# Forward attention scores in PSUM tiles of three banks instead of two

## The chip, the cores and the metric

The kernel runs on one core of a Trainium2 chip. The metric is the device time of one execution in microseconds. The engines that matter here are TensorE (PE), VectorE (DVE), ScalarE (ACT), GpSimd (POOL) and the DMA queue of SyncE (SP). Each engine works through its own list of instructions in order; semaphores hold an instruction back until what it needs is there. PSUM, into which PE writes, has eight banks of 512 float32 numbers per partition.

## The reference

One transformer block with conditioned layer norms, forward and backward in one launch. Attention has 32 heads of 16 numbers over 2048 tokens; the dense block has an inner width of 1792 and a squared ReLU.

```python
h = _layernorm(x) * (1 + ca) + sa
x = x + ga * _A_ref(h, A_wqkv, A_wo)          # softmax attention
h = _layernorm(x) * (1 + cb) + sb
x = x + gb * _B_ref(h, B_w1, B_b1, B_w2, B_b2)
...
scores = jnp.einsum('bhqd,bhkd->bhqk', q, k) * Dh ** (-0.5)
p = _softmax(scores, axis=-1)
o = jnp.einsum('bhqk,bhkd->bhqd', p, v)
```

The kernel returns the output and the gradients of nine inputs.

## The kernel before

Up to about 42 us the kernel prepares norms and the first projections. Then comes the forward loop, to 995 us, which the change is in. After it come the last chunk's dense block and the backward attention loop (exponentials at L1600), which are not touched.

**The forward loop** runs over `NF` = 512 units, `funits`: four chunks of 512 queries (`qc`), in each of them eight groups of four heads (`hg`), in each of these 16 key tiles of 128 keys (`kt`). Sixteen units with the same chunk and heads are called a group here; there are 32.

`fscore(u)` makes the scores of one unit. Each head has its 16 dimensions in its own 32 rows of the tiles `kt_sb` and `qt_sb`, so one head is one matmul on a row group of PE (L576), with a score tile of 128 keys by 512 queries, one PSUM bank. Two heads share a PSUM tile `psST` of two banks; ACT then takes the exponential of the 1024 columns (L578) into `ET`. There are three `psST` tiles in turn, and four `ET` tiles of a whole unit each.

`fpv(u)` multiplies the exponentials with the values, four matmuls side by side into the columns of one tile `oacc` (L592). It is called two units behind the scores. At the last key tile DVE copies `oacc` out to `ostage` (L596).

**What else goes on in the loop** is put between the units by hand. All engines' instructions stand in the order in which the code calls them. In the first 130 units or so a table, `plan`, puts in the key, query and value projections (L812, L826, `key_norm`, `token_tile`) for later chunks and heads. From unit 140 on `step(u)` takes one piece of a generator, `dense_chunk`, which runs the dense block forward and backward for a finished chunk of queries: products with four matmuls a piece at L410 (14 pieces), L424 (14), L446 (16), L500 (16, closed by a bias matmul at L505), L532 (4), transposes at L348, and the chains of weight gradients at L233. All of these share one PSUM tile of one bank, `pm`, which DVE empties (L412, L427, L457, L507 and L510, L536, L251) before the next product may begin. `steady` gives PE two filler matmuls (L615) in units with no product. PE's order in a unit thus is: four scores, four PV matmuls, a product or fillers.

Loads of the next group's keys and queries go out on POOL's queue one per unit from key tile 4 on (`fload`); other transfers go out on SP's queue at unit numbers (`later`).

PSUM is full: three `psST` of two banks, one `oacc`, one `pm`.

Of the kernel before, what the change touches and what calls it, by code (L numbers as in the profile page):

```python
# [14 lines left out]
AF = mybir.ActivationFunctionType  # L15
ALU = mybir.AluOpType
AX = mybir.AxisListType
BF = dt.bfloat16
F32 = dt.float32

P = 128
# [7 lines left out]
SCALE = 0.25  # L29
# [5 lines left out]
def kernel(  # L35
# [8 lines left out]
    TT = n // P  # L44
# [8 lines left out]
    PE = nc.tensor  # L53
    DVE = nc.vector
    ACT = nc.scalar
# [91 lines left out]
    with ExitStack() as ph:  # L147
# [1 line left out]
        ffw = ph.enter_context(tc.tile_pool(name="ffw", bufs=1))  # L149
        cb = ph.enter_context(tc.tile_pool(name="phMc", bufs=1))  # L150
        att = ExitStack()
        ework = att.enter_context(tc.tile_pool(name="phCe", bufs=4))
        b2row = ffw.tile([1, D], BF, name="b2row")
        racc = ffw.tile([P, 5, D], F32, name="racc")
        pools = {}
# [24 lines left out]
        def later(lag, f, *args):  # L180
            due.append((unit[0] + lag, f, args))

        def run_due(everything=False):
            i = 0
            while i < len(due):
                if everything or due[i][0] <= unit[0]:
                    _, f, args = due.pop(i)
                    f(*args)
                else:
                    i += 1  # L190
# [363 lines left out]
        funits = [(qc, hg, kt) for qc in range(QC) for hg in range(HG) for kt in range(TT)]  # L554
        fh, fe, fcur, fdone, dense = {}, {}, {}, [], []

        def fload(qc, hg):
            i = hg % 2
            kt_sb, qt_sb = kts[i], qts[i]
            rows = list(row_loads(kt_sb, qkT_st[1], hg, slice(0, n)))  # L560
            rows += row_loads(qt_sb, qkT_st[0], hg, slice(512 * qc, 512 * qc + 512), m_st)
            for i, (to, fro) in enumerate(rows):
                later(i, POOL.dma_start, to, fro)
            run_due()
            fh[qc, hg] = (qt_sb, kt_sb)

        def fscore(u):
            qc, hg, kt = funits[u]
            qt_sb, kt_sb = fh[qc, hg]
            ET = ework.tile([P, 4, 512], BF, name="ET", tag="ET")  # L570
            fe[u] = ET
            for pair in range(2):
                ps = pools["s"].tile([P, 2, 512], F32, name="psST", tag="psST")
                for hi in range(2):
                    r = 32 * (2 * pair + hi)
                    PE.matmul(ps[:, hi, :], kt_sb[r:r + 32, kt * P:(kt + 1) * P], qt_sb[r:r + 32, :],  # L576
                              start=True, stop=True, tile_position=(r, 0))
                ACT.activation(ET[:, 2 * pair:2 * pair + 2, :], ps[:], AF.Exp, scale=SCALE)  # L578

        def fpv(u):  # L580
            qc, hg, kt = funits[u]
            if kt == 0:
                fcur["o"] = pools["o"].tile([P, 512], F32, name="oacc", tag="oacc")
                if hg == 0:
                    fcur["rr"] = ework.tile([H, 512], F32, name="rrows", tag="rrows", bufs=1)
                    fcur["ou"] = ework.tile([P, 4, HG, P], BF, name="O_un", tag="O_un", bufs=1)
            oacc = fcur["o"]
            ET = fe.pop(u)
            for hq in range(4):
                h = hg * 4 + hq  # L590
                lhsT = vaug[:, kt].rearrange("p h c -> p (h c)")[:, h * (DH + 1):h * (DH + 1) + 32]
                PE.matmul(oacc[32 * hq:32 * hq + 32, :], lhsT, ET[:, hq, :],  # L592
                          start=(kt == 0), stop=(kt == TT - 1), tile_position=(0, 32 * hq), skip_group_check=True)
            if kt == TT - 1:
                ostage = ework.tile([P, 512], F32, name="ostage", tag="ostage", bufs=1)
                DVE.tensor_copy(ostage[:], oacc[:])  # L596
                obf = ework.tile([P, 512], BF, name="obf", tag="obf", bufs=2)
                if u == NF - 1:
                    fcur["last"] = ostage
                    return  # L600
                if hg == HG - 1:
                    DVE.tensor_copy(obf[:], ostage[:])
                else:
                    POOL.tensor_copy(obf[:], ostage[:])
                for hq in range(4):
                    h = hg * 4 + hq
                    later(2, sp, fcur["rr"][h:h + 1, :], ostage[32 * hq + 16:32 * hq + 17, :])
                later(3, sp, fcur["ou"][:, :, hg, :], obf[:], True)
                if hg == HG - 1:
                    fdone.append((u + 7, qc, fcur["rr"], fcur["ou"]))  # L610

        def steady(u):
            if 0 <= u < NF and funits[u][2] < TT - 1:
                for _ in range(2):
                    PE.matmul(fcur["o"][0:DH, :], zeros[:], identb.unsqueeze(1).to_broadcast([P, 4, P]), start=False, stop=False,  # L615
                              tile_position=(0, 0), skip_group_check=True)
# [497 lines left out]
        NF = len(funits)  # L1114
# [4 lines left out]
        def step(u):  # L1119
            nonlocal wait, turn  # L1120
            ripe = dwq and not open_group[0] and u >= dwq[0][0]
            if wait > 0 or not dense:
                wait = max(0, wait - 1)
                if ripe:
                    next_chain()
                return
            if ripe and turn and ((len(dwq) > 14 and fqueue) or dwq[0][3]):
                turn = 0
                next_chain()
                return  # L1130
            turn = 1
            w = next(dense[0], -1)
            if w == -2:
                next_chain()
            elif w == -1:
                dense.pop(0)
                run_due(True)
                if not fqueue:
                    loads["L"] = chunk_loads(QC - 1)
            else:  # L1140
                wait = w
# [6 lines left out]
        plan_tasks()  # L1148
        stages = [*range(4, 14), *range(4), 30, 31, *range(14, 25)]
        with ExitStack() as ph2:  # L1150
            pools["s"] = ph2.enter_context(tc.tile_pool(name="psS", bufs=3, space=bass.MemoryType.PSUM))
            pools["o"] = ph2.enter_context(tc.tile_pool(name="psO", bufs=1, space=bass.MemoryType.PSUM))
            pools["mm"] = ph2.enter_context(tc.tile_pool(name="psM", bufs=1, space=bass.MemoryType.PSUM))
            with tc.manual_schedule(engines={PE.engine, ACT.engine, DVE.engine, SP.engine, POOL.engine}):
                fh[0, 0] = (qts[0], kts[0])
                for u in range(NF + 2):
                    unit[0] = u
                    run_due()
                    if u < NF:
                        if funits[u][2] == 4 and u + TT < NF:  # L1160
                            fload(*funits[u + TT][0:2])
                        fscore(u)
                    if 2 <= u:
                        fpv(u - 2)
                    if u % 4 == 2 and u // 4 < len(stages):
                        later_stage(stages[u // 4])
                    if u % 4 == 0 and 18 <= u // 4 < 32:
                        turn_weights(u // 4 - 18)
                    count, begun_group = products[0], open_group[0]
                    for f, args in plan.pop(u, ()):  # L1170
                        f(*args)
                    if u < NF - 4:
                        step(u)
                    elif dwq and u >= NF - 2:
                        next_chain()
                    if products[0] == count and not (begun_group or open_group[0]):
                        steady(u - 2)
                    if u >= NF - 7 and "L" in loads and "O" not in loads["L"]:
                        early_finish()
                    if u == NF:  # L1180
                        tiny = wk.tile([P, 1], F32, name="tiny", tag="tiny", bufs=1)
                        ACT.activation(tiny[:], onesf[:, 0:1], AF.Sqrt)
                    if not dense and fqueue and fdone and u - 2 >= fdone[0][0]:
                        fqueue.pop(0)
                        qc, rr, ou = fdone.pop(0)[1:]
                        ffinish(qc, rr, ou, chunk_loads(qc))
                while dense:
                    unit[0] += 1
                    run_due()
                    step(unit[0])  # L1190
# [357 lines left out]
    with ExitStack() as ph:  # L1548
        tpool = ph.enter_context(tc.tile_pool(name="phIt", bufs=3))
        ework = ph.enter_context(tc.tile_pool(name="phIe", bufs=4))  # L1550
# [193 lines left out]
        with tc.manual_schedule(engines={PE.engine, ACT.engine, DVE.engine, SP.engine, POOL.engine}):  # L1744
# [4 lines left out]
            for b in range(NU // 4 + 3):  # L1749
                toks, bank = order_t if on_pe(b - 1) else order_n  # L1750
                for tok in toks:
                    c, i = tok[0], int(tok[1:] or 0)
# [43 lines left out]
    with ExitStack() as ph:  # L1796
# [174 lines left out]
        with tc.manual_schedule(engines={PE.engine, ACT.engine, DVE.engine}):  # L1971
            for i in range(2):
                rsums.append(pst.tile([P, D], F32, name="rsumJ", tag="ptq"))
            for t in range(TT):
# [4 lines left out]
                if t in (3, 5, 7, 9):  # L1979
                    i = 4 + (t - 3) // 2  # L1980
# [11 lines left out]
            for b in range(3):  # L1992
                for ic in range(DC):
                    dwqkv(b, ic)
                    i = b * DC + ic
# [77 lines left out]
```

## Time and profile before

| what | value |
|---|---|
| median of three runs | 2478.51 us (2475.77 to 2486.17) |
| profiled execution | 2479.05 us, span 2477.3 us |
| mean granted TensorE clock | 0.986 |
| PE busy | 2320.3 us (94% of the span) |
| ACT busy | 2302.8 us (93%) |
| DVE busy | 1834.7 us (74%) |
| forward loop, first to last exponential | 42.4 to 994.6 us |
| in the loop (42 to 995 us): ACT, PE, DVE busy | 942.4, 867.9, 472.3 us |

The span is the time from the first to the last instruction in the profile; the rest of the execution's time lies around it. A line of a group of instructions gives: source line, engine, operation, what it writes and reads, shapes, how many; behind the first bar the busy time in us (overlapping instructions counted once) and the mean duration of one in ns; behind the second bar the idle time of the engine just before them in us, and what ended most of it. A line of a timeline gives: start in us from the span's beginning, duration, engine, source line, operation, tiles and shapes, how many were merged into the line, and in brackets the idle time before it with what ended it. [...]

### The profile page before, as it was taken

Reading aid. Unit: us, or ns where it says so; the run is one execution under the profiler, and the core shown is the slowest. Engines: PE = TensorE matmul, PEld = TensorE weight load, DVE = VectorE, ACT = ScalarE, POOL = GpSimd, SP = SyncE. Lnnn points to the kernel's source line nnn. Section 1 sums busy time; section 2 is a strip of 40 time slices with the busy share of each in tenths; the row PEclk is TensorE's granted clock in tenths of the full one; section 3 lists DMA queues with packets and bytes.
Section 4 is the critical chain, followed back from the end, with each engine's and each line's share of the span. In section 5 each row is a group of like instructions: output and inputs, shape, how many; then the busy total and the mean of one; then the engine's idle time right before and its main releaser. Section 6 shows DMA issues by size and latency. Waiting matters only on the chain.

```text
span 2477.3 us, 49960 instructions
## 1 busy us (share of the span) xinstructions
PE 2320.3 (94%) x19020; PEld 780.1 (31%) x19020; DVE 1834.7 (74%) x2375; ACT 2302.8 (93%) x3560; POOL 487.5 (20%) x660
## 2 busy tenths in 40 slices
PE   8899899989998998899999999999999999999999
PEld 3232233323322332442233233332232323323344
DVE  6555353455445554578999999999999999999985
ACT  7999999999999999639999999999999999999964
POOL 2211222432544352101111101101011010110100
PEclk9999999999998999999999999999999999999999
DMA  4478453266647765979999999999999999999995
GB/s 148 125 173 179 143 142 101 84 172 134 91 93 162 150 134 104 248 225 170 196 203 210 192 209 198 205 201 206 206 211 192 209 201 200 207 191 217 201 265 179
DMA packets 1190335, 438.22 MB, mean 177 GB/s; under 512 B 1068107, under 2 KB 1161225, under 8 KB 1189582
## 3 DMA queue, kind: packets, MB, share of 16 engines
q1 hardware_dynamic: 1153246, 389.87, 79.9%
q0 software_dynamic: 19872, 27.09, 6.7%
q10 hardware_dynamic: 16976, 18.07, 2.9%
q8 instruction: 149, 2.44, 0.4%
q14 instruction: 92, 0.75, 0.1%
HBM read 98.30 MB, written 70.80 MB: 68 GB/s over the span
## 4 chain that ended last, share of the span: by engine, by line
ACT 41%; PE 38%; issue 8%; DVE 8%; DMA 2%; ACTq 1%; POOL 0%; DVEq 0%; POOLq 0%
ACT E_u L1600 25%; ACT ET L578 12%; PE dqacc L1702 4%; PE psST L576 3%; PE psS_A L1594 3%; PE pm L233 2%; PE accVK L1675 2%; ACT dsT L1787 2%; PE psS_B L1594 2%; PE oacc L592 2%; PE pm L500 2%; PE pdh L1895 2%; PE pm L424 2%; PE psS_C L1594 2%; PE pm L410 2%
## 5 line engine op out<-in xcount | busy, mean ns | idle before, releaser
L1616 DVE TENSOR_TENSOR dS_u<-psD_u,E_u 128x1024 bf16<-128x1024 f32 x1024 | 1185.2, 1216 | 70.8 <-PE psD_u L1614 26.2
L578 ACT ACTIVATE ET<-psST 128x1024 bf16<-128x1024 f32 x1024 | 942.0, 1245 | 13.7 <-PE psST L576 13.3
L1600 ACT ACTIVATE E_u<-psS_A 128x512 bf16<-128x512 f32 x768 | 508.3, 662 | 10.8 <-PE psS_C L1594 8.1
L1600 ACT ACTIVATE E_u<-psS_B 128x512 bf16<-128x512 f32 x768 | 501.5, 653 | 10.1 <-PE psD_u L1614 3.0
L1614 PE MATMUL psD_u<-iv,ido 32*128 32x512 bf16 x2048 | 408.3, 386 | 1.2 <-DVE dS_u L1616 1.1
L576 PE MATMUL psST<-qt_sb,kt_sb 32*128 32x512 bf16 x2048 | 315.8, 386 | 45.5 <-ACT ET L578 40.7
L1600 ACT ACTIVATE E_u<-psS_C 128x512 bf16<-128x512 f32 x512 | 333.3, 651 | 2.3 <-PE psS_B L1594 0.9
L1594 PE MATMUL psS_B<-ik,iq 32*128 32x512 bf16 x768 | 294.2, 383 | 11.0 <-ACT E_u L1600 3.7
L1594 PE MATMUL psS_A<-ik,iq 32*128 32x512 bf16 x768 | 292.6, 381 | 11.4 <-DVE dwlast L237 0.9
L1723 POOL TENSOR_TENSOR dQacc<-dQacc,dqtmp 128x512 f32<-128x512 f32 x64 | 81.2, 1268 | 851.7 <-ACT dqtmp L1718 851.7
L1594 PEld LDWEIGHTS <-iq 32*128 32x128 bf16 x2048 | 130.4, 91 | 314.3 <-issue 296.9
L1675 PE MATMUL accVK<-dS_u,qz 128*32 128x512 bf16 x2048 | 213.4, 388 | 0.4 <-DVE dS_u L1616 0.2
L592 PE MATMUL oacc<-ET,vaug 128*32 128x512 bf16 x2048 | 206.9, 394 | 3.9 <-DVE ostage L596 3.9
L1684 PE MATMUL accVK<-E_u,dOs_tok 128*16 128x512 bf16 x2048 | 203.5, 386 | 0.0
L1594 PE MATMUL psS_C<-ik,iq 32*128 32x512 bf16 x512 | 193.5, 378 | 4.3
L576 PEld LDWEIGHTS <-kt_sb 32*128 32x128 bf16 x2048 | 85.1, 91 | 327.9 <-issue 308.0
L1702 PE MATMUL dqacc<-dsT,KS_tok 128*32 128x512 bf16 x2048 | 146.5, 383 | 14.8 <-DMA dsT<-dS_u 1.4
L251 DVE COPY part<-pm 128x512 f32<-128x512 f32 (+2 forms) x106 | 65.1, 614 | 119.3 <-PE pm L233 115.6
L1787 ACT ACTIVATE dsT<-ptT 128x1024 bf16<-128x1024 bf16 x126 | 142.6, 1132 | 6.5 <-PE ptT L1648 5.8
L1614 PEld LDWEIGHTS <-ido 32*128 32x128 bf16 x2048 | 105.5, 91 | 102.1 <-issue 96.0
L1675 PEld LDWEIGHTS <-qz 128*32 128x32 bf16 x2048 | 58.6, 94 | 177.6 <-issue 162.6
L592 PEld LDWEIGHTS <-vaug 128*32 128x32 bf16 x2048 | 53.1, 93 | 122.1 <-issue 122.1
(419 smaller groups left out, 2668.4 us busy)
## 6 DMA issues: line engine op xcount, KB each, us to landing
p_st<-part POOLq DMA_DIRECT2D x36, 256.0 KB, 4.7
kt_sb<-qkT_st POOLq DMA_DIRECT2D x124, 64.0 KB, 2.9
wA<-in_B_w_dram SPq DMA_DIRECT2D x28, 256.0 KB
wB<-w1T_st SPq DMA_DIRECT2D x21, 256.0 KB
wA<-w2T_st SPq DMA_DIRECT2D x21, 256.0 KB
wB<-in_B_w_dram SPq DMA_DIRECT2D x21, 256.0 KB
p_st<-part POOLq DMA_DIRECT2D x28, 192.0 KB, 4.8
p_st<-part SPq DMA_DIRECT2D x18, 256.0 KB
```

The lines of the kernel that those rows point to most:

```text
L576: PE.matmul(ps[:, hi, :], kt_sb[r:r + 32, kt * P:(kt + 1) * P], qt_sb[r:r + 32, :], start=True, stop=True, tile_position=(r, 0))
L578: ACT.activation(ET[:, 2 * pair:2 * pair + 2, :], ps[:], AF.Exp, scale=SCALE)
L592: PE.matmul(oacc[32 * hq:32 * hq + 32, :], lhsT, ET[:, hq, :], start=(kt == 0), stop=(kt == TT - 1), tile_position=(0, 32 * hq), skip_grou ...
L1594: PE.matmul(psS[:], st["q"][r:r + 32, qt * P:(qt + 1) * P], st["k"][r:r + 32, kc * 512:kc * 512 + 512], start=True, stop=True, tile_positi ...
L1600: ACT.activation(bst[u][0][:, hq, :], sst.pop((u, hq))[:], AF.Exp, scale=SCALE)
L1614: PE.matmul(psD[:, hi, :], st["do"][r:r + 32, qt * P:(qt + 1) * P], st["v"][r:r + 32, kc * 512:kc * 512 + 512], start=True, stop=True, til ...
L1616: DVE.tensor_tensor(dS_u[:, 2 * pair:2 * pair + 2, :], psD[:], E_u[:, 2 * pair:2 * pair + 2, :], ALU.mult)
L1675: PE.matmul(cur["vk"][32 * hq:32 * hq + 32, :], hst[hg]["qz"][:, qt, hq, :], bst[u][1][:, hq, :], start=(qt == 0), stop=False, tile_positi ...
L1684: PE.matmul(acc[32 * hq:32 * hq + DH, :], dOs_tok[:, qt, (hg * 4 + hq) * DH:(hg * 4 + hq + 1) * DH], E_u[:, hq, :], start=False, stop=(qt ...
L1702: PE.matmul(acc[32 * hq:32 * hq + 32, :], KS_tok[:, kc * 4 + kt, h * DH:h * DH + 32], tT[:, :, hq * 4 + kt, :], start=(kt == 0), stop=(kt ...
L1723: POOL.tensor_tensor(dst2, dst, tmp[:], ALU.add)
L1787: ACT.activation(dst, pt[:], AF.Identity)
```

## The change

The score tiles get three banks, and there are two of them. The scores of a group are 16 x 4 = 64 banks in order of key tile and head; they are cut into 22 slots, twice ten of three banks and one of two. A slot has one PSUM tile, one exponential and one `ET` tile of three banks (five of these in turn). A slot may hold heads of two neighbouring key tiles. The loop calls `fscore` once in every unit, and once more at the end of the units of key tiles 1, 4, 7, 10, 12 and 15, behind that unit's product. `fpv` of a unit is called inside `fscore`, once the unit's last slot is two slots back, at most one per slot; four of its matmuls read the unit's four heads from one or two `ET` tiles.

```diff
-        ework = att.enter_context(tc.tile_pool(name="phCe", bufs=4))
+        ework = att.enter_context(tc.tile_pool(name="phCe", bufs=5))
...
-        def fscore(u):
-            qc, hg, kt = funits[u]
+        widths = ([3] * 10 + [2]) * 2
+        first_tile = [sum(widths[:j]) for j in range(len(widths))]
+        doubles = (1, 4, 7, 10, 12, 15)
+        slot_ends = {}
+        fnext = {"slot": 0, "pv": 0}
+
+        def fscore():
+            s = fnext["slot"]
+            fnext["slot"] = s + 1
+            g, j = divmod(s, len(widths))
+            qc, hg, _ = funits[g * TT]
             qt_sb, kt_sb = fh[qc, hg]
-            ET = ework.tile([P, 4, 512], BF, name="ET", tag="ET")
-            fe[u] = ET
-            for pair in range(2):
-                ps = pools["s"].tile([P, 2, 512], F32, name="psST", tag="psST")
-                for hi in range(2):
-                    r = 32 * (2 * pair + hi)
-                    PE.matmul(ps[:, hi, :], kt_sb[r:r + 32, kt * P:(kt + 1) * P], qt_sb[r:r + 32, :],
-                              start=True, stop=True, tile_position=(r, 0))
-                ACT.activation(ET[:, 2 * pair:2 * pair + 2, :], ps[:], AF.Exp, scale=SCALE)
+            w = widths[j]
+            ET = ework.tile([P, 3, 512], BF, name="ET", tag="ET")
+            ps = pools["s"].tile([P, 3, 512], F32, name="psST", tag="psST")
+            for i in range(w):
+                kt, hq = divmod(first_tile[j] + i, 4)
+                r = 32 * hq
+                PE.matmul(ps[:, i, :], kt_sb[r:r + 32, kt * P:(kt + 1) * P], qt_sb[r:r + 32, :],
+                          start=True, stop=True, tile_position=(r, 0))
+                fe.setdefault(g * TT + kt, []).append(ET[:, i, :])
+                slot_ends[g * TT + kt] = s
+            ACT.activation(ET[:, 0:w, :], ps[:, 0:w, :], AF.Exp, scale=SCALE)
+            if fnext["pv"] < NF and len(fe.get(fnext["pv"], ())) == 4 and slot_ends[fnext["pv"]] <= s - 2:
+                fpv(fnext["pv"])
 
         def fpv(u):
+            fnext["pv"] = u + 1
...
-                PE.matmul(oacc[32 * hq:32 * hq + 32, :], lhsT, ET[:, hq, :],
+                PE.matmul(oacc[32 * hq:32 * hq + 32, :], lhsT, ET[hq],
...
-            pools["s"] = ph2.enter_context(tc.tile_pool(name="psS", bufs=3, space=bass.MemoryType.PSUM))
+            pools["s"] = ph2.enter_context(tc.tile_pool(name="psS", bufs=2, space=bass.MemoryType.PSUM))
...
-                        fscore(u)
-                    if 2 <= u:
-                        fpv(u - 2)
+                        fscore()
+                    elif u < NF + 1:
+                        while fnext["pv"] < NF - 1:
+                            fpv(fnext["pv"])
+                    else:
+                        fpv(NF - 1)
...
-                        steady(u - 2)
+                        steady(fnext["pv"] - 1)
+                    if u < NF and funits[u][2] in doubles:
+                        fscore()
```

## The prediction

> **What bounds the kernel now.** I read the page first (busy rows, then groups), then the waits inside the forward loop (42 to 995 us of the span), then the timeline of single units. A unit is one 128-key tile for four heads; the loop has 512 of them, 32 groups (head group and chunk) of 16. Nothing outside the loop is touched.
>
> ```profile
> PE   8899899989998998899999999999999999999999
> DVE  6555353455445554578999999999999999999985
> ACT  7999999999999999639999999999999999999964
> ```
>
> These rows of the page are tenths busy in 40 slices of 62 us. In slices 2 to 16 ACT is full, PE nearly, DVE half.
>
> ```profile
> L578 ACT ACTIVATE ET<-psST 128x1024 bf16<-128x1024 f32 x1024 | 942.0, 1245 | 13.7 <-PE psST L576 13.3
> L576 PE MATMUL psST<-qt_sb,kt_sb 32*128 32x512 bf16 x2048 | 315.8, 386 | 45.5 <-ACT ET L578 40.7
> ```
>
> ACT's 1024 exponentials fill 942 of 952 us; it idled 13.3 us for scores, and PE waited 40.7 us for ACT to free score tiles. ACT sets the loop, PE follows closely. The mean of 1245 ns is not the price of an exponential, since neighbours overlap. The price is read from PE's timeline where the loop runs on ACT alone:
>
> ```profile
> 262.51 0.39 PE L576 MATMUL psST<-qt_sb,kt_sb 32*128 32x512 bf16 x2 [0.37 <-ACT ET L578]
> ...
> 264.34 0.39 PE L576 MATMUL psST<-qt_sb,kt_sb 32*128 32x512 bf16 x2 [0.37 <-ACT ET L578]
> ...
> 266.18 0.39 PE L576 MATMUL psST<-qt_sb,kt_sb 32*128 32x512 bf16 x2 [0.37 <-ACT ET L578]
> ```
>
> The same score pair waits for ACT every 1.834 us, so one 1024-column exponential costs 0.917. For half the width I take the backward loop's unbroken ACT stretch:
>
> ```profile
> 1508.22 0.63 ACT L1600 ACTIVATE E_u<-psS_B 128x512 bf16<-128x512 f32 x1
> ...
> 1510.61 0.69 ACT L1600 ACTIVATE E_u<-psS_A 128x512 bf16<-128x512 f32 x1
> ```
>
> Ends lie 2.45 us and five instructions apart: 0.490 for 512 columns. Hence 0.427 per 512 columns, 0.063 fixed per instruction, and 0.917 + 0.427 = 1.344 for 1536 columns (estimate: no PSUM exponential of that width is in the trace).
>
> **Part 1, fewer exponentials: -20.2 us.** A group now has 32 x 0.917 = 29.34 us of exponentials; afterwards 20 x 1.344 + 2 x 0.917 = 28.71. Times 32: 320 fixed costs of 0.063 saved, 20.2 us, and the pace of a unit falls from 1.834 to 1.795. Bounds for the 1536-column price: 1.280 (no fixed cost) and 1.5 x 0.917 = 1.375 (nothing saved, 0 us in place of -20.2); I take 1.344, on the line through both measured widths.
>
> [...]
>
> **Part 2, the slack between PE and ACT.** A score tile may be refilled from 0.05 us after the exponential that empties it, and must be begun 0.49 before ACT needs it: after a stall, scores begun at 785.54 let ACT start at 786.03. The slack is (tiles - 1) exponentials less 0.54: now 2 x 0.917 - 0.54 = 1.29 us, afterwards 1.344 - 0.54 = 0.80. PE gets less even, too. A score burst takes 0.325 before the next kind of matmul starts, whether two or four matmuls are in it (they start 3 ns apart, on different row groups), so I take it for three; PV 0.326; four products 4 x 0.215 + 0.096 = 0.956. A unit with a product and one burst is 1.607 of PE work. In the built order the six extra slots of a group stand behind the products of key tiles 1, 4, 7, 10, 12 and 15, against the next unit's slot. So in a run of three units PE lags ACT by 3 x (1.607 - 1.344) = 0.79 and then gains it back: it fits into 0.80 with nothing over. A unit in which PE waits longer costs ACT time that is covered now.
>
> **Part 3, stages that give back.** (a) The product loop at L410:
>
> ```profile
> 805.95 0.40 PE L576 MATMUL psST<-qt_sb,kt_sb 32*128 32x512 bf16 x4
> 806.05 0.75 DVE L412 TENSOR_SCALAR rT<-pm,b1col 128x512 bf16<-128x512 f32 x1 [0.66 <-PE pm L410]
> 806.27 0.40 PE L592 MATMUL oacc<-ET,vaug 128*32 128x512 bf16 x4
> ...
> 806.86 1.02 PE L410 MATMUL pm<-h2T,wA 128*128 128x512 bf16 x4 [0.18 <-DVE rT L412]
> ...
> 807.81 0.39 PE L576 MATMUL psST<-qt_sb,kt_sb 32*128 32x512 bf16 x4
> ```
>
> The one product tile goes PE, DVE, PE in 1.866 us whatever ACT does; an extra burst hides in that wait (0.31 + 0.215 + 0.65 = 1.18 us from the last product matmul to the next, against 1.866 - 0.645 = 1.22 by way of the eviction). So 42 units (14 in each of three chunks) do not get faster: 42 x 0.039 = 1.6 us given back. (b) In the alternating L424 and L233 products units last 1.804 and 1.884, also paced by eviction: 64 units, 2.5 us. (c) L500, where two DVE reads free the tile late:
>
> ```profile
> 474.98 0.69 DVE L507 TENSOR_TENSOR gfprod<-pm,g_c 128x512 bf16<-128x512 f32 x1 [6.53 <-PE psST L576]
> ...
> 475.59 0.68 DVE L510 TENSOR_TENSOR ftmp<-pm,modbc 128x512 bf16<-128x512 f32 x1
> ...
> 476.32 1.02 PE L500 MATMUL pm<-wB,sT 128*128 128x512 bf16 x4 [0.40 <-DVE ftmp L510]
> ...
> 477.27 0.40 PE L576 MATMUL psST<-qt_sb,kt_sb 32*128 32x512 bf16 x4
> ```
>
> From 474.56 to 477.27 PE gives ACT nothing new; then three units of 1.63, 1.63 and 1.37 catch up, and ACT never runs dry (12 units in 22.04 us, 1.837 each). Walking the new slots through those 12 units with the prices above (next product 2.07 behind the last one at each tile change), ACT idles 0.36, 0.26, 0.61, 0.61 and 0.27, together 2.1 us, because 2.71 - 1.34 is beyond 0.80 and the extra slots take PE's time for catching up. 48 units: 8.4 us. The four L532 units that follow in each chunk are paced by eviction at up to 1.99: 1.0 us. (d) L446, five-unit cycles with one gap of 2.2: the same walk gives 0.8 us of idle in 15 units; 56 units: 3.0. (e) The first 51 units, where key, norm and value products wait on evictions: half the gain lost, 1.0. (f) ACT's own 13 stalls, where PE stands behind DVE or a transfer: two lie at the start; at each of the other 11 the slack is 0.49 less, and PE stands somewhere in its run, so 0 to 0.49 each; I take 0.4, near the end that full runs make: 4.4. Sum given back: 1.6 + 2.5 + 8.4 + 1.0 + 3.0 + 1.0 + 4.4 = 21.9.
>
> **Part 4, edits at nothing.** The exponential's ET tile is one of five with three banks instead of four with four; its readers, the PV of a unit whose last slot is two back, are issued behind the score two slots earlier, so it is free over an exponential before it is needed. If it were not, all later exponentials and the scores behind them would queue, 1.3 us a time. PV keeps its two units' distance and never waits for ACT, since the score ahead of it waited for the same exponential. SP's and POOL's orders are the old ones; the next group's key and query loads land in 2.9 us (median), the last of them is issued four units (7.3 us) ahead, and that lead shrinks by 4 x 0.04 us. The filler matmuls stay as many.
>
> **Sum.** 2479.05 (the profiled execution: span 2477.3 and 1.75 around it) - 20.2 + 21.9 = 2480.8, so 2481. That execution lies 0.5 us above the median of 2478.51; 0.5% of it, 12 us, is about what a measurement of this kernel can tell from no change.
>
> **Rivals.** *Slack suffices, faster.* If PE makes up at L500, L446 and the stalls what it loses, only the eviction-paced 1.6 + 2.5 + 1.0 go back: 2479.05 - 20.2 + 5.1 = 2464. For it: ACT is never dry at L500 now. Against it: 0.79 in 0.80. Chance 0.19.
>
> *The run overshoots, slower.* If a burst of three tiles costs PE or ACT's start 0.1 us more than a pair does, every run of three product units ends some 0.3 late instead of just in time. That decides from bursts over 0.33 on. Some 380 units carry products, about 220 of them outside (a) to (d): 82 runs, of which a late one leaves the next half relieved, 0.2 each: 16 us more, 2497. For it: nothing is left over in the window, and only bursts of two and of four have been seen. Against it: those cost the same. Chance 0.24. [...]
>
> *Three scores do not run side by side, much slower.* At 0.215 more per slot a group of products needs 22 x 0.54 + 16 x (0.326 + 0.956) = 32.4 of PE against 29.3 now; over some 18 such groups 56 us: 2535. Against it: four start within 10 ns of each other at 805.95. Chance 0.04.
>
> *The fixed cost is larger, much faster.* An exponential after idle lasts 1.02 from start to end (786.03), 0.164 over its columns; were that the price, 320 x 0.164 = 52 saved, 2449. Against it: the 1.834 cycle. [...] Chance 0.02.
>
> **How the numbers follow.** The forecast keeps 0.51. Faster by over 0.5% (below 2466) are the first and last rival, 0.21; slower by over 0.5% (above 2491) the two middle ones, 0.28; within it 0.51, with its own range of 2467 to 2490 (terms c, d and f between half and one and a half). The range reaches from the first rival to the second, and up to the bound where a wide exponential saves nothing (2501): 2463 to 2500.
>
> **What would show it.** Ends of wide exponentials 1.34 apart. ACT's idle on psST in the loop rising from 13 to some 30 us, most of it at L500 and behind stalls. L410 units still 1.87. The light units around 261 us at 1.80. The last exponential within 5 us of 994.6. A loop that ends before 982 refutes part 3; one after 1006, or score bursts over 0.33, shows the second or third rival.

## The result, and the profile after

The changed kernel takes 2502.71 us in the median of seven runs (2492.82 to 2506.6), the kernel before 2478.51 (2472.83 to 2489.76). The ratio is 1.008, with a 95% interval of 1.005 to 1.0109: slower by 0.5 to 1.1%. The profiled execution took 2506.1 us with a span of 2504.3, so it lies in the upper part of the seven; it is 27.05 us above the profiled execution of before. It also has the lowest mean granted clock of the seven, 0.979; the four at 0.985 to 0.988 took 2492.82 to 2502.71.

All of this is in the forward loop. From the first to the last exponential it lasts from 41.6 to 1023.8 us, 982.1 us against 952.2, which is 29.9 more; what follows lasts 1480.5 us against 1482.6, and the loop begins 0.8 earlier.

The busy rows of the changed kernel's page, tenths in 40 slices of 63 us, with the granted TensorE clock:

```profile
PE   8888789888988898899999999999999999999999
ACT  7999999989999999646999999999999999999964
PEclk9999899999999999999999999999999999999999
```

ACT, which was at 9 in slices 2 to 16, now drops to 8 in the ninth slice, its light stretch at the loop's end is a slice longer, and PE has more slices at 8. The fifth digit of the clock is an 8.

The two groups of the loop on the same page; behind the second bar stands the engine's idle time:

```profile
L589 ACT ACTIVATE ET<-psST 128x1536 bf16<-128x1536 f32 (+1 forms) x704 | 933.5, 1443 | 52.1 <-PE psST L585 49.9
L585 PE MATMUL psST<-qt_sb,kt_sb 32*128 32x512 bf16 x2048 | 278.1, 393 | 81.9 <-ACT ET L589 75.0
```

ACT idled 49.9 us for scores where it had been 13.3, and PE waited 75.0 us for ACT where it had been 40.7. Both wait longer for each other: with two tiles each has less in hand when the other is late. The list of waits in the loop (42 to 1025 us; total, times, longest) says how often:

```profile
PE psST L585 <- ACT ET L589: 75.0, 154, 1.0
ACT ET L589 <- PE psST L585: 49.9, 91, 3.5
```

ACT ran dry 91 times instead of 13 (gaps over 0.15 us). The longest case is 3.5 us as before, so what is new is many short gaps.

Where the loop runs on ACT alone, the timeline of the changed kernel shows the price of the wide exponential:

```profile
262.38 0.39 PE L585 MATMUL psST<-qt_sb,kt_sb 32*128 32x512 bf16 x3 [0.43 <-ACT ET L589]
...
263.73 0.39 PE L585 MATMUL psST<-qt_sb,kt_sb 32*128 32x512 bf16 x3 [0.20 <-ACT ET L589]
...
265.07 0.39 PE L585 MATMUL psST<-qt_sb,kt_sb 32*128 32x512 bf16 x2 [0.20 <-ACT ET L589]
...
266.41 0.40 PE L585 MATMUL psST<-qt_sb,kt_sb 32*128 32x512 bf16 x3 [0.95 <-ACT ET L589]
```

Each slot waits for the release of a tile, 1.35, 1.34 and 1.34 us apart. Over all ends of back-to-back exponentials the interval is 1.3425 for 1536 columns and 0.9165 for 1024.

With these prices the loop's account can be drawn up. I call lost time what the ends of the exponentials lie apart beyond the price of each. Before, 13.6 us were lost in the loop; afterwards 64.2. So 20.2 us were saved, 50.6 more were lost, and the difference is 30. The clock records divide the lost time: before, 7.2 us fell into stretches in which TensorE was granted half its clock (with 2 us behind each) and 6.4 outside; afterwards 21.3 and 42.9. By the 22 slots of a group, counted from 0, lost time stands mostly at slots 2, 6, 10, 13, 14 and 21 (4.3, 7.8, 7.4, 7.4, 7.1 and 8.5 us of the 64.2): five of these are extra slots, issued behind a product.

### The profile page after: what moved, and what is told of

Same layout as the page of the kernel before. It is cut to its first block, busy times and chain, and to the rows that moved or that the text cites. A ratio compares the mean times of both kernels' runs of the same rounds, so it can differ in the third digit from the quotient of the medians.

```text
span 2504.3 us, 49831 instructions
## 1 busy us (share of the span) xinstructions
PE 2299.9 (92%) x19020; PEld 775.5 (31%) x19020; DVE 1833.5 (73%) x2375; ACT 2293.4 (92%) x3240; POOL 487.8 (19%) x660
## 5 line engine op out<-in xcount | busy, mean ns | idle before, releaser
L589 ACT ACTIVATE ET<-psST 128x1536 bf16<-128x1536 f32 (+1 forms) x704 | 933.5, 1443 | 52.1 <-PE psST L585 49.9
L585 PE MATMUL psST<-qt_sb,kt_sb 32*128 32x512 bf16 x2048 | 278.1, 393 | 81.9 <-ACT ET L589 75.0
L585 PEld LDWEIGHTS <-kt_sb 32*128 32x128 bf16 x2048 | 77.3, 91 | 336.9 <-issue 326.1
```

What stands on the lines that cost most here:

```text
L585: PE.matmul(ps[:, i, :], kt_sb[r:r + 32, kt * P:(kt + 1) * P], qt_sb[r:r + 32, :], start=True, stop=True, tile_position=(r, 0))
L589: ACT.activation(ET[:, 0:w, :], ps[:, 0:w, :], AF.Exp, scale=SCALE)
```

## The experiments

Three theories were put to the test. *Slack*: two tiles leave 0.80 us where three left 1.29, and extra slots behind products bring PE late by more. *Clock*: the half-speed stretches, twelve in place of five in the loop, cost the time. *Burst*: a second score burst in a unit, behind the product, costs PE time by itself.

**Two pair tiles.** The kernel before, with its third score tile taken away:

```diff
-            pools["s"] = ph2.enter_context(tc.tile_pool(name="psS", bufs=3, space=bass.MemoryType.PSUM))
+            pools["s"] = ph2.enter_context(tc.tile_pool(name="psS", bufs=2, space=bass.MemoryType.PSUM))
```

> The kernel before with two score tiles of two banks instead of three; nothing else. Slack theory: two tiles leave 0.917 - 0.54 = 0.38 us between PE and ACT instead of 1.29, so every unit with a product (1.607 us between score bursts) leaves ACT dry; the unit becomes about 2.1 us in the 380 product units, 2550 to 2600 us in all, ACT idle on scores over 70 us. Clock theory (the loss is half-speed windows of TensorE): nothing but the share of those windows counts, so near 2480 unless they become more. Burst theory (the extra score bursts cost PE time): bursts are as many as before, so 2480.

Measured: 2576.58 us, ratio 1.0396 (1.0337 to 1.0455), from two executions of 2567.23 and 2585.94; the profile is of the faster. The two groups on its page:

```profile
L578 ACT ACTIVATE ET<-psST 128x1024 bf16<-128x1024 f32 x1024 | 968.2, 1031 | 82.9 <-PE psST L576 76.6 <-ACT ET L578 0.2
L576 PE MATMUL psST<-qt_sb,kt_sb 32*128 32x512 bf16 x2048 | 373.1, 390 | 108.9 <-ACT ET L578 100.7 <-DVE vP L831 1.8
```

The same exponentials, and ACT idles 76.6 us for scores in place of 13.3; the loop lasts 1047.6. By the rule of the prediction the slack here is 0.917 - 0.54 = 0.38. Slack of 1.29, 0.80 and 0.38 goes with 13.6, 64.2 and 109.0 us lost: the number of tiles alone costs this much, and the wider tile buys back part of what the missing third tile costs.

**Extra slot first.** The changed kernel, with the second slot of a double unit scored right behind the first, so ahead of the unit's product:

```diff
                         fscore()
+                        if funits[u][2] in doubles:
+                            fscore()
...
-                    if u < NF and funits[u][2] in doubles:
-                        fscore()
```

> The changed kernel with the six extra slots of a group called right behind the unit's first slot, ahead of its product, instead of behind the product. Slack theory: the largest lag of a run falls from 0.79 to about 0.53 against 0.80, and at L410 the extra burst lies in the wait for the eviction; ACT's idle in the loop falls from 50 to 25 us and the time to about 2480. Clock theory: same number of half-speed windows, so as the changed kernel, 2492 to 2506. Burst theory: same number of bursts, so as the changed kernel.

Measured: 2487.64 us, ratio 1.0046 (1.0028 to 1.0064); the loop is 963.4. Of the 64.2 us lost, 18.8 are back by nothing but the order in which the same work stands on PE (15.1 by the medians; 12.2 of the 18.8 lie outside half-speed stretches). A time of about 2480 was expected. What remains gathers at slots 12 and 13, 20.2 us of 45.4, ahead of the extra slot of key tile 10.

**Four fillers.** The changed kernel with four filler matmuls in a unit without a product, so that PE works more:

```diff
-                for _ in range(2):
+                for _ in range(4):
```

> The changed kernel with four filler matmuls in place of two in units without a product (0.43 us more of PE work in such a unit, 1.61 between bursts, still under ACT's pace). Clock theory: PE is busier in the light stages, the half-speed windows in the loop fall from 12 towards the 5 of the kernel before, and 8 to 15 us come back. Slack theory: the product stages stay as they are; light units now lag as product units do, so the same or up to 5 us slower.

Measured: 2510.42 us, ratio 1.0127 (1.01 to 1.0154). There are six half-speed stretches in its loop (37.5 us) in place of twelve (64.9), and yet the loop is longer, 990.2, with 72.3 us lost. The 8 to 15 us that the clock theory expected back did not come: half as many stretches gained nothing that the fillers' own PE time did not take again. Since the fillers cost time of their own, this run alone does not price the clock; the executions at equal clock that are compared further down do. The granted clock is higher with more fillers, 0.987 in this profile against 0.979 (0.9865 against 0.985 in the median of the executions).

**Split pairs.** The kernel before, three tiles of two banks, with the second pair of a unit scored behind the product, where the changed kernel has its extra slots:

```diff
                         fscore(u, (0,))
...
+                    if u < NF:
+                        fscore(u, (1,))
```

> The kernel before, three tiles of two banks, but the second pair of a unit is scored behind the unit's product instead of right after the first pair: the bursts become as scattered as in the changed kernel (more so), the tiles and exponentials stay. Slack theory: the lag inside a unit is 1.607 - 0.917 = 0.69, within the 1.29 of three tiles; only stages where PE itself sets the pace (L500) pay for the extra burst, 3 x 0.215 us in four units: 2484 to 2490. Burst theory: 512 more bursts cost more than the 192 of the change did, 20 us or more: over 2500.

Measured: 2474.36 us, ratio 0.999 (0.9974 to 1.0005), lost time 11.6 us. With three tiles a score burst behind the product adds nothing to the loop (2484 to 2490 was expected even by the slack theory), and the burst theory, by which 512 more bursts cost 20 us or more, falls. That a burst takes PE time which only the slack of three tiles hides is not excluded.

**First and nine.** Extra slot first, and the double unit of key tile 9 in place of 10:

```diff
-        doubles = (1, 4, 7, 10, 12, 15)
+        doubles = (1, 4, 7, 9, 12, 15)
```

> extra_slot_first with the extra slot of key tile 10 moved to key tile 9, so that the extra slots stand 3, 3, 2, 3, 3, 2 units apart instead of 3, 3, 3, 2, 3, 2 with a two-bank slot ahead of the long gap. Slack theory: ACT's lost time at slots 12 to 14 of a group, 20 of 45 us in extra_slot_first, falls to the 8 of the other half of the group; 2472 to 2478. If only the number of tiles mattered and not the lag, no change: 2487.

Measured: 2479.54 us, ratio 1.0007 (0.9991 to 1.0022). The groups on its page:

```profile
L589 ACT ACTIVATE ET<-psST 128x1536 bf16<-128x1536 f32 (+1 forms) x704 | 928.7, 1452 | 31.2 <-PE psST L585 29.0
L585 PE MATMUL psST<-qt_sb,kt_sb 32*128 32x512 bf16 x2048 | 283.2, 389 | 68.9 <-ACT ET L589 62.7 <-DVE vP L845 1.8
```

The time is just above the 2472 to 2478 that were expected. ACT's idle time for scores is 29.0 us, the loop 956.4, lost time 38.5 (11.9 in half-speed stretches). A unit is timed here, and in what follows where nothing else is said, from the start of its PV matmuls to that of the next unit's. Two stages are back near the pace of 1.795: units 51 to 155 last 1.815 instead of 1.854 and those at L446 1.788 instead of 1.852; L410 stays slow at 1.936. So 25.7 of the 29.9 us were a matter of where the six extra slots stand. This kernel has the tiles of the change and the time of the kernel before.

**Nine only.** The changed kernel with key tile 9 for 10 alone, the extra slots still behind the products.

> The changed kernel with key tile 9 in place of 10 among the extra slots, which stay behind the products. Slack theory: the worst lag of a group falls from about 1.0 to 0.75 of a unit; ACT's lost time at slots 12 to 14 falls from 17 to some 6 us, so 8 to 12 us faster than the changed kernel, 2490 to 2495. Clock theory: no change, 2492 to 2506 as the changed kernel's runs spread.

Measured: 2499.47 us, ratio 1.008 (1.0054 to 1.0106); the loop is 976.3. The slots 12 to 14 lose some 10 us where they lost 17, but other slots lose more, and its interval overlaps that of the change; 2490 to 2495 was expected. Behind the products the choice of key tile settles little; most of the gain above comes from the place ahead of the product.

**Mid product.** First-and-nine's double units, with the extra slot between the second and the third matmul of the unit's product.

```diff
+                    if ic == 2:
+                        halfway()
...
-                    if u < NF and funits[u][2] in doubles:
-                        fscore()
+                    halfway()
```

> The changed kernel with key tile 9 for 10, and the extra slot called in the middle of the unit's product, between its second and third matmul (behind the product where it has no such middle). Extra slots then stand about two thirds of a unit behind the slot before, close to the 0.73 of a unit that ACT needs. Slack theory: the most even supply of the three places, lag at most some 0.45 us; 2465 to 2478, and below extra_slot_first. Burst theory: an extra change of kind in PE per extra slot, 192 x 0.1 = 19 us of PE time, slower than extra_slot_first.

Measured: 2505.79 us, ratio 1.0115 (1.0091 to 1.0139), loop 983.3 in the profile, which is of the longest of six executions. The expectation was missed: units at L410 rise to 2.034. The burst stands inside the product, so the eviction that the next product waits for starts later: of the 39 intervals from product to product, the 24 without such a burst last 1.87 and the 15 with one 2.29 or more. Only one of these 15 holds a wait of PE for ACT, so here it is the burst itself that costs. That was a first sign of what the L410 loop is sensitive to.

**Half products.** In both kernels the dense products of the loop are cut to the first and the last matmul of each four; the outputs of the dense block are therefore not those of the reference, and the times serve only to show PE with less work. The core of the edit, the same in both:

```diff
-                for ic in range(DC):
+                for ic in (0, DC - 1):
```

> The kernel before with the dense block's products inside the forward loop cut to the first and last matmul of each four (the other two are left out, so the sums are incomplete). PE has 0.43 us less in each such unit. Slack theory: the loop was set by ACT, so only the eviction-paced stages and stalls gain: 2468 to 2478.

> The changed kernel with the same half products left out (the first and last matmul of each four stay). The gap between score bursts falls from 1.607 to 1.177 us, below ACT's 1.344. Slack theory: runs no longer lag, the 20 us of fixed cost come out: 12 to 20 us faster than half_products_before. If wide exponentials brought nothing, or if the loss came from the new order itself or from the clock: as slow against half_products_before as the change was, 10 to 25 us slower.

Measured: 2478.27 us (ratio 1.001, 0.9991 to 1.0028) with three tiles, 2479.98 (1.0008, 0.9986 to 1.003) with two wide ones; the loops last 951.8 and 953.9. The change's loss is gone when PE has less to do: it was PE that could not follow. But the gain of 12 to 20 us that was expected for two wide tiles did not come. The clock rows, first that of the kernel before, then of the changed one, each with half products:

```profile
PEclk9999999999997999999999999999899999999999
```

```profile
PEclk9999999989997998999999999999999999999999
```

With less work PE's clock fell more often: 11 half-speed stretches in the first loop (61.4 us), 19 in the second (109.2 us). With three tiles 13.2 us are lost, 12.6 of them in those stretches; with two, 35.9, of them 24.6 there. That is 0.21 and 0.23 us lost for each us at half speed, so a stretch costs about the same with either number of tiles; with two there were more of them, and outside them 11.2 us were lost in place of 0.6. Single executions at the same clock show that part of the expected gain is there: at 0.973 to 0.977 four with three tiles took 2478.05 to 2485.19 us, three with two tiles 2471.94 to 2474.67. But with two tiles the median clock of the ten executions is 0.9705, with three 0.978.

**PV behind.** First-and-nine, with the PV of a double unit behind the product, so that only the two score bursts stand ahead of it.

```diff
                         if funits[u][2] in doubles:
                             fscore()
+                        else:
+                            ripe_pv()
...
+                    if u < NF:
+                        ripe_pv()
```

> first_and_nine, with the PV matmuls of a unit with an extra slot called behind its product instead of between its slots. In the eviction-paced products (L410, L424) the two bursts and their wait for ACT then have 1.22 us from product to product to themselves, of which they need 0.31 + 0.215 + 0.325 = 0.85: a wait of up to 0.37 for ACT no longer lengthens the loop from product to eviction to product. Slack theory: L410 units fall from 1.94 to 1.87 to 1.89, L424 and L233 likewise, 4 to 6 us in all: 2472 to 2477. If the wait ahead of the product is not what slows these stages, L410 stays at 1.94 and the time at 2480.

Measured: 2516.27 us, ratio 1.0156 (1.0137 to 1.0175), where 2472 to 2477 was expected; the loop is 992.0 in the profile, which is of the longest execution (2530.01). A new wait took the place of the old one. The PE timeline at a group's start:

```profile
843.34 0.40 PE L608 MATMUL oacc<-ET,vaug 128*32 128x512 bf16 x4
843.67 0.39 PE L585 MATMUL psST<-qt_sb,kt_sb 32*128 32x512 bf16 x3
845.31 0.40 PE L608 MATMUL oacc<-ET,vaug 128*32 128x512 bf16 x4 [1.25 <-DVE ostage L612]
```

The last PV of a group is late here (843.34), the next group's first PV needs the single `oacc`, and PE stands 1.25 us until DVE has copied it out. In the loop PE waits so 30 times, 28.7 us, against 4 times and 4.0 us in first-and-nine. Slots 4 and 5 lose 37.9 us over the groups. The PV of key tile 1's double unit closes that window, so it was put back:

**PV behind, inner.** As above, with the PV of key tile 1 between its two slots.

```diff
+                        if funits[u][2] not in doubles[1:]:
+                            ripe_pv()
                         if funits[u][2] in doubles:
                             fscore()
```

> pv_behind, with the PV matmuls of key tile 1's unit back between its two slots, so that the group's last PV is not late and the next group's first PV does not wait for the copy of the one output tile (in pv_behind 1.25 us at a group's end, and 38 of 74 us of ACT's lost time at slots 4 and 5 behind it). Slack theory: that loss goes, L410 stays at about 1.90, the rest as in first_and_nine: 2472 to 2480. If late PV matmuls cost ACT otherwise (its ET tiles), over 2490.

Measured: 2482.29 us, ratio 1.003 (1.0016 to 1.0044), loop 959.8; 2472 to 2480 was expected. Slots 4 and 5 are down to 9.0 us, and the waits for `oacc` to 4, which bears out that wait. The aim at L410 was missed. The 11 intervals there with nothing but two bursts between two products do last 1.87, in place of 1.93 with a PV between the bursts. But the PV that was put behind a product now stands in the next interval, with that unit's burst and PV: 12 such intervals last 1.95 where a burst and a PV lasted 1.87. Over all 39 the mean is 1.902, in first-and-nine 1.895. Units timed by their PV matmuls mislead here, since the edit moves these; by the ends of the exponentials L410 is the same in both (1.897 and 1.898). The 3.4 us that this loop is longer lie, by the same ends, mostly at L446 (2.2) and L500 (1.7), less some 0.8 that the first units gain. No version with two wide tiles was faster than the kernel before.

## Why the prediction was right or wrong

The forecast was 2481 with a range of 2463 to 2500. The median lies 2.7 us above the range, 2478.51 times the ratio of 1.008 just inside (2498); slower by over 0.5% was given 0.28, and the forecast itself, no change, did not come true.

**Part 1 was right.** 1.344 was predicted and 1.3425 measured, so the 20.2 us are in the loop.

**The rule of part 2 held.** Scores are begun 0.50 before ACT can start (830.14 and 830.64 in the trace, 0.49 predicted), and a burst of three takes 0.325 until the next kind of matmul (832.41 to 832.74 below), as was taken from bursts of two and four. Lost time rises (13.6, 64.2 and 109.0 us) as the slack falls through 1.29, 0.80 and 0.38. What was wrong was to let the run of three units fit 0.79 into 0.80 and to call the rest free. The sum of part 3, 21.9 us, was too small by 28.7: 50.6 were given back. By its terms, with units timed from PV to PV (timed by the ends of the exponentials single terms come out up to 1.7 us otherwise); they come to 44.5, and some 6 us lie in units of no term:

*(a) L410, 1.6 us: failed.* Its units were to stay at 1.87 "whatever ACT does" and last 1.976, 1.854 before (from product to product 1.96, 1.87 before); with the 0.039 that each was to gain, 6.8 us are given back. The timeline of the changed kernel at such a unit:

```profile
832.41 0.39 PE L585 MATMUL psST<-qt_sb,kt_sb 32*128 32x512 bf16 x3
...
832.74 0.40 PE L606 MATMUL oacc<-ET,vaug 128*32 128x512 bf16 x4
...
833.32 1.02 PE L410 MATMUL pm<-h2T,wA 128*128 128x512 bf16 x4 [0.19 <-DVE rT L412]
...
834.28 0.39 PE L585 MATMUL psST<-qt_sb,kt_sb 32*128 32x512 bf16 x3
834.39 0.75 DVE L412 TENSOR_SCALAR rT<-pm,b1col 128x512 bf16<-128x512 f32 x1 [0.66 <-PE pm L410]
834.82 0.39 PE L585 MATMUL psST<-qt_sb,kt_sb 32*128 32x512 bf16 x3 [0.15 <-ACT ET L589]
...
835.15 0.40 PE L606 MATMUL oacc<-ET,vaug 128*32 128x512 bf16 x4
...
835.48 1.04 PE L410 MATMUL pm<-h2T,wA 128*128 128x512 bf16 x4
```

The product at 833.32 has one burst and one PV ahead of it and waits for its eviction. From there to the next product, at 835.48, are 2.16 us. The eviction is done at 835.14, but PE is not there: the extra burst of 834.28 uses up the tile in hand, the next unit's burst must wait until ACT releases the other (834.82), and PV follows. The prediction had the extra burst hide in the wait for the eviction (1.18 in 1.22) and put no wait for ACT in between. In the whole stage, 23 intervals with a single burst still last 1.87 in the mean, but 14 with two bursts and one PV last 2.09, and eight of these hold a wait for ACT (0.04 to 0.67 us); the six without last 1.87, just as the prediction had it. In the kernel before, all 39 such intervals last 1.86 to 1.93 and none holds a wait. So the sum 1.18 was right and the freedom to issue was wrong. In first-and-nine the 14 intervals with an extra slot hold no wait, but the order burst, PV, burst, and last 1.93; in the last experiment 11 intervals have two bursts alone and are back at 1.87, but the 12 that take over their PV last 1.95.

*(b) L424 and L233, 2.5 us: failed in the same way.* The 64 units last 1.908 instead of 1.841 and give back 6.9. From product to product, 39 intervals with one burst last 1.85 in the mean, 22 with two 2.04; nine of these hold a wait for ACT and last 2.14.

*(c) and (d), L500 and L446: right in size.* L500 gave back 6.0 of 8.4 predicted, L446 4.2 of 3.0; these two had been walked through slot by slot. The L532 units gave back 3.1 where 1.0 was put.

*(e) the first units, 1.0, and the 105 light units after them, nothing: failed.* They gave back 4.0 and 4.4. In first-and-nine they are at 1.805 and 1.815, so what they lost was mostly the place of the extra slots, though the light units hold few full products. A part is the clock. The timeline of the changed kernel ahead of the lines shown first:

```profile
258.59 0.61 PE L585 MATMUL psST<-qt_sb,kt_sb 32*128 32x512 bf16 x3
...
259.30 9.32 ACT L589 ACTIVATE ET<-psST 128x1536 bf16<-128x1536 f32 x7 [0.48 <-PE psST L585]
...
259.53 0.92 PE L629 MATMUL oacc<-identb,zeros 128*16 128x512 bf16 x2
```

Scores of 0.61 instead of 0.39 mark half speed (the granted clock here is 0.50); ACT stands 0.48 for them, in a unit without a product.

*(f) ACT's stalls, 4.4: too small.* Units 251 to 283 and their counterparts in the other chunks, where most stalls lie, gave back 9.1. How much of it is the clock and how much the slack isn't settled.

**What no term had: the clock.** Of the 50.6 us, 14.1 fall into half-speed stretches and what follows them; that is where they fall, not proof that the clock caused all of it. The other 36.5 fall outside; in first-and-nine 16.3 of these are back and 9.4 of the 14.1, so the place of the slots bears on both. The single executions tell slack and clock apart: in every kernel the time rises as the mean granted clock falls, some 14 us for 0.01 in the 82 executions of the kernel before that ran beside the experiments. At clocks of 0.985 to 0.988, 46 of these have a median of 2476.9 us; four of the changed kernel have 2494.5, four of extra slot first 2486.0, six of first-and-nine 2478.8, and three with four fillers 2511.2. So at the same clock the change costs some 18 us, and the place of the slots gives back 16 of them. The clock is a smaller part, which differs from execution to execution.

**The rivals.** The second, slower at 2497, came true in its place and nearly in its time, but not by the condition that it named: bursts over 0.33 or a later start were not needed. Its argument that "nothing is left over in the window" was the right reason to give it more weight than the forecast. That its price of 16 us came so near was luck in part: by the prediction's own terms about 220 of the 380 product units lie inside (a) to (d), not outside, so its way of counting leaves some 160 units, 60 runs and 12 us. The third (2535) is refuted: three scores start 3 ns apart and cost 0.325. The mark that was set for these two, a loop that ends after 1006, was passed with 1023.8. The first rival's reason, that PE makes up what it loses, is what the kernel before can do with three tiles; with two and half products it nearly does so outside the half-speed stretches (11.2 us lost there).

A gap that keeps coming back on ACT, the engine that sets the loop, is in the trace now: 91 gaps and 49.9 us, against 13 and 13.3 before.

## What to carry to other kernels

Two large buffers in place of three small ones save fixed cost (0.063 us an instruction here), but the slack between producer and consumer, reckoned here as (tiles - 1) times the consumer's instruction less a turnaround of 0.54 us, falls with them (1.29 to 0.80 us here); compare it with the producer's longest run of full units, and where it just fits, as 0.79 did here, expect it not to. An in-order engine that must wait for a buffer in the middle of a unit also delays what stands behind the wait, here the next product (begun at 835.48, its tile free at 835.14) and its eviction, so a stage that is paced by another loop is not immune: L410 went from 1.854 to 1.976 us a unit. If the buffers must be few, issue the extra work ahead of the long piece and not behind it: here the same instructions in another order gave back 25.7 of 29.9 us. And when an edit moves the instructions by which a stage is timed, time it by others.

## What the runs showed of the hardware

Two matmuls of 512 columns one after the other start 0.215 us apart (median of the 126 pairs within the products at L410, in the kernel before), though the profile shows each with 0.38.

In the loop of the changed kernel the granted clock falls to half (0.50 in the clock records) in twelve stretches: seven of 3.41 us, three of 6.83 and two of 10.24, together 64.9 us, which is 19 times 3.41; the 109.2 us of half products with two tiles are 32 times that. It falls without a long pause of PE: PE was between 63% and 81% busy in the 6.8 us ahead of eleven of the twelve, in nine of these with no gap over 0.96 us, and ahead of none of the twelve was a gap over 2.6 us. In the profiles less work on PE went with more stretches in the loop (5 before, 11 with half products; 12 after, 19 with half products), more fillers with fewer (6). What they cost did not hang on the number of tiles: with full products 7.2 us were lost in 23.9 us at half clock with three tiles and 21.3 in 64.9 with two, about 0.3 each; with half products 12.6 in 61.4 and 24.6 in 109.2, about 0.2 each.
